# Windowed attention with a mixture of attention experts: tie mask, softmax path, one score block and the issue order

## The chip, the core and the metric

The kernel runs on one core of a Trainium2 chip. The metric is the time of one execution on the device in microseconds; of several runs the median counts. TensorE, VectorE, ScalarE and GpSimd work side by side on tiles in SBUF, TensorE writes to eight banks of PSUM, and SyncE issues nearly all transfers between HBM and SBUF. In the profile these are PE, DVE, ACT, POOL and SP; PEld is TensorE's weight load.

## What is computed

The first part is attention of 8 batches with 8 heads, 576 positions and 64 columns a head, in which each query sees its own and the 63 positions before it. Its output, 512 columns a position, goes into a mixture of four causal attention experts. A gate picks the two best experts for each position and weighs them. The core of the reference in outline:

```python
# first part: q, k, v are (8, 8, 576, 64)
scores = scale * np.matmul(q, k.transpose(0, 1, 3, 2))
mask = (rel >= 0) & (rel < window)            # window = 64
attn = softmax(np.where(mask, scores, -1e9))
x = np.matmul(attn, v)                        # to (8, 576, 512)

# second part
logits = x @ w_gate                           # 4 experts
topk = np.argpartition(-logits, 2, axis=-1)[..., :2]
w = softmax of the two chosen logits
for e in range(4):
    q, k, v = x @ wq[e], x @ wk[e], x @ wv[e]
    a = softmax(causal(scale * (q @ k.T)))
    out += w of e (0 where e is not chosen) * (a @ v @ wo[e])
```

## The kernel before

**First part.** The work is cut into 576 tiles, each of 64 queries of a pair of heads, and eight tiles make a unit u; there are 36 units. `s1_qk` (L379) multiplies queries by keys (TensorE, plain fp32), and builds the softmax in a tile `sm1_u`: ScalarE and a predicated copy on VectorE bring the scores from PSUM to SBUF, VectorE takes the maximum into `st1_u`. From there two paths lead on. A biased unit (odd u below 12, L408) lets ScalarE take the exponential of each of the eight tiles with its own bias, with the sum read from ScalarE's accumulator. Every other unit has GpSimd add the negative maximum, ScalarE take one exponential of the whole, and VectorE reduce the sum. VectorE's reciprocal and GpSimd's product follow. `s1_t` (L424) transposes the result on TensorE (t1), masks it into pt1; `s1_av` multiplies by the values (o1) and writes the output as two fp32r tiles, XH (rounded) and XL (the rest).

**Second part.** It runs in 16 halves (b, pr), a batch and a pair of experts. `s2_v` projects values and gate logits (v2ps), `s2_gate` (L598) builds the gate weights, `s2_k` and `s2_q` (L646, L657) project keys and queries (kps, qps). A product of this part is three fp32r products, hi·hi, hi·lo and lo·hi (`three`, L569). From the projected keys come KT, a high part that ScalarE copies and a low part that VectorE subtracts, and KF, the first 64 columns in plain fp32; queries likewise give QT and QF. `s2_mm` (L676) computes the scores in four steps k. Query block i holds queries 128i-64 to 128i+63, and step 0 holds block 1 with 192 keys and block 2 with 320 keys. The two experts of a pair lie in different halves of the partitions, so their matmuls use different rows of the array. The first 64 queries go through QF and KF in plain fp32 (`s2_mm0`). `s2_soft` takes the minimum, the exponential and the weights, `s2_t` transposes on VectorE and moves blocks by 16 transfers, `s2_av_mm` multiplies by the values (o2), `s2_o` by wo (ops), and the result leaves.

**The gate's ties.** For each position and each pair of experts (e, f) `g4[:, 0]` says whether f's logit is greater than e's. The row sums are the ranks. Where two logits are equal, the lower number wins: `g4[:, 1]` says whether they are equal, GpSimd multiplies it by a constant `below` (1 where f < e) and adds it to `g4[:, 0]`. There are 12 calls: eight for four blocks of 128 positions at once (64 columns), four for a single block (16 columns).

**What sets the order.** Every engine call is recorded as a numbered operation, a matmul block as one, and issued in the order of a table of numbers, LIST (L29). So one table sets the order on every engine, SyncE's loads included. BANKS (L170) names the PSUM bank of each tile in the order of recording, and SLOTS (L178) the SBUF slot of each `sm1`, `ft` and `out` tile. All instructions come out of the same helper and carry its line, L218:

```python
for n in LIST:
    for call, args, kw in self.ops[n]:
        call(*args, **kw)
```

## Time and profile before

| | |
|---|---|
| time, median of 3 runs | 408.18 us (407.21 to 409.73) |
| profiled execution | 406.65 us |
| its span | 404.9 us |
| granted TensorE clock | 0.999 |
| TensorE busy | 395.0 us, 98% |
| VectorE busy | 304.9 us, 75% |
| ScalarE busy | 270.2 us, 67% |
| GpSimd busy | 266.4 us, 66% |

The span is the time from the first to the last recorded instruction or transfer of the profiled execution; 1.75 us lie around it. The shares are of the span. Matmuls are pipelined and overlap in the records, so the mean duration of a matmul is longer than the distance from one start to the next; where a step's price is meant, a row that holds a block of known count is read. A plain fp32 matmul stands in the records as two passes, an fp32r matmul as one. In the chain of waits and the list of waits, a name behind an arrow is what the waiting engine waited for.

### The profile page before, as it was taken

To read this page: it belongs to the slowest core of one execution; us is meant where nothing else is said; L and a number is where in the kernel's file an instruction comes from. 1 tells how busy PE (TensorE), PEld (TensorE's weight loads), DVE (VectorE), ACT (ScalarE), POOL (GpSimd) and SP (SyncE) were. 2 spreads that over 40 slices of the span, in tenths; PEclk is the share of its full clock that TensorE was granted. 3 is DMA by queue.
4 is the path that set the end of the run, shared out by engine and by line. 5 is a ranking of instruction groups with operands and counts; after the bars stand their busy time and mean duration, and the time that the engine had idled before them with its cause. 6 is when DMAs were issued, how large, how long until landed. Compare 5 with 4: busy or idle time off the path is not lost.

```text
span 404.9 us, 14099 instructions
## 1 busy us (share of the span) xinstructions
PE 395.0 (98%) x5316; PEld 357.1 (88%) x5316; DVE 304.9 (75%) x989; ACT 270.2 (67%) x960; POOL 266.4 (66%) x465
## 2 busy tenths in 40 slices
PE   7799999999999999999999999999999999999995
PEld 6589989999888999889988999989998999988884
DVE  4899999978987688767886868968786748386632
ACT  4889888758576585946676575757657473748842
POOL 3756658897879666977677767887668663506300
PEclk9999999999999999999999999999999999999999
DMA  7998335565867573687957574378646630645024
GB/s 223 344 398 298 122 91 204 142 202 156 266 210 230 117 233 137 152 267 210 295 141 196 154 211 197 89 188 314 169 122 163 168 78 22 145 129 145 2 90 159
DMA packets 34132, 72.70 MB, mean 180 GB/s; under 512 B 6544, under 2 KB 11152, under 8 KB 34064
## 3 DMA queue, kind: packets, MB, share of 16 engines
q1 hardware_dynamic: 33408, 71.14, 58.2%
q8 instruction: 42, 0.69, 0.7%
q10 hardware_dynamic: 656, 0.66, 0.6%
q14 instruction: 26, 0.21, 0.2%
HBM read 39.85 MB, written 9.44 MB: 122 GB/s over the span
## 4 chain that ended last, share of the span: by engine, by line
PE 90%; DMA 3%; ACT 3%; DVE 2%; SPq 1%; issue 0%
PE o L218 20%; PE s L218 16%; PE ops L218 13%; PE v2ps L218 12%; PE qps L218 12%; PE kps L218 12%; PE t L218 4%; DMA v<-in_vW_dram 2%; ACT sm L218 2%; DMA q<-in_qT_dram 1%; DVE p L218 1%; SPq L218 1%; PE warm L218 1%; DVE pt L218 1%; ACT ft L218 0%
## 5 line engine op out<-in xcount | busy, mean ns | idle before, releaser
L218 POOL TENSOR_SCALAR_AFFINE_SELECT pt<-ft 64x512 f32<-64x512 f32 x126 | 83.2, 664 | 35.4 <-ACT ft L218 24.5
L218 POOL TENSOR_SCALAR p<-p,r,g 128x448 f32<-128x448 f32 (+3 forms) x135 | 83.6, 632 | 18.0 <-DVE r L218 15.8
L218 ACT ACTIVATE p<-p,r 128x320 f32<-128x320 f32 (+4 forms) x135 | 78.2, 585 | 13.1 <-DVE r L218 12.9
L218 PE MATMUL o<-pt,v 128*64 128x64 f32 (+2 forms) x1776 | 80.2, 248 | 0.8 <-DVE gt L218 0.3
L218 PEld LDWEIGHTS o<-pt,v 128*64 128x64 f32 x1776 | 68.0, 138 | 13.4 <-issue 1.7
L218 POOL TENSOR_TENSOR sm<-sm,st 128x512 f32<-128x512 f32 x66 | 68.3, 1044 | 13.5 <-DVE st L218 6.6
L218 DVE STREAM_TRANSPOSE st<-p 128x128 f32<-128x128 f32 (+5 forms) x126 | 60.7, 515 | 7.7 <-DMA pt<-st 5.1
L218 DVE CUSTOM_DVE_ANT_0 p<-s,causal 128x320 f32<-128x320 f32 (+2 forms) x120 | 53.4, 484 | 7.4 <-PE s L218 6.9
L218 DVE TENSOR_REDUCE st<-sm 128x8 f32<-128x512 f32 x66 | 44.3, 678 | 5.8 <-ACT sm L218 5.0
L218 PE MATMUL s<-kt,qt 64*128 64x320 f32 (+3 forms) x480 | 41.7, 315 | 0.0
L218 PE MATMUL qps<-xh,wqhi 128*128 128x320 f32 (+1 forms) x128 | 39.1, 306 | 0.0
L218 PE MATMUL s<-k,q 64*64 64x128 f32 (+1 forms) x1116 | 36.2, 267 | 2.3 <-DMA q<-in_qT_dram 2.1
L218 PE MATMUL kps<-xh,wkhi 128*128 128x320 f32 (+1 forms) x128 | 38.2, 299 | 0.0
L218 PE MATMUL qps<-xl,wqhi 128*128 128x320 f32 (+1 forms) x128 | 37.7, 294 | 0.0
L218 PE MATMUL qps<-xh,wqlo 128*128 128x320 f32 (+1 forms) x128 | 37.6, 294 | 0.0
L218 PE MATMUL kps<-xh,wklo 128*128 128x320 f32 (+1 forms) x128 | 37.6, 294 | 0.0
L218 PE MATMUL kps<-xl,wkhi 128*128 128x320 f32 (+1 forms) x128 | 37.6, 294 | 0.0
L218 PE MATMUL v2ps<-wvhi,xh 128*128 128x260 f32 x128 | 37.3, 291 | 0.0
L218 DVE COPY_PREDICATED sm<-own,s 128x256 f32<-128x256 uint8 x72 | 29.5, 438 | 9.0 <-ACT sm L218 7.9
L218 PE MATMUL v2ps<-wvhi,xl 128*128 128x260 f32 x128 | 36.1, 282 | 0.0
L218 PE MATMUL v2ps<-wvlo,xh 128*128 128x260 f32 x128 | 36.1, 282 | 0.0
L218 PEld LDWEIGHTS s<-kt,qt 64*128 64x128 f32 x480 | 34.6, 186 | 1.7 <-issue 0.4
(126 smaller groups left out, 939.8 us busy)
## 6 DMA issues: line engine op xcount, KB each, us to landing
v<-in_vW_dram SPq DMA_DIRECT2D x28, 576.0 KB, 6.2
pt<-st SPq DMA_DIRECT2D x112, 116.0 KB, 2.3
pt<-st SPq DMA_DIRECT2D x112, 80.0 KB, 2.1
out_dram<-out SPq DMA_DIRECT2D x32, 256.0 KB, 2.5
q<-in_qT_dram SPq DMA_DIRECT2D x28, 288.0 KB, 5.4
k<-in_kT_dram SPq DMA_DIRECT2D x28, 288.0 KB, 5.2
v<-in_vW_dram SPq DMA_DIRECT2D x3, 320.0 KB, 7.1
out_dram<-out SPq DMA_DIRECT2D x7, 128.0 KB, 2.5
```

Source lines behind the costliest of these rows:

```text
L218: call(*args, **kw)
```

## The change

1. **Gate.** `is_equal` becomes `is_ge`, and the two GpSimd operations give way to one predicated copy on VectorE: where `lower`, a byte copy of `below` that is made once, is set, `g4[:, 0]` is overwritten with the result of `is_ge`.
2. **Softmax path.** The biased units are 1, 3 and 5 instead of 1, 3, 5, 7, 9 and 11. Units 7, 9 and 11 take the path with the add on GpSimd, one exponential and the reduction on VectorE.
3. **Scores of queries 64 to 191** (block 1, 192 keys): one plain fp32 product from QF and KF instead of three fp32r products from QT and KT, for each expert. QF and KF grow from 64 to 192 columns, QT shrinks from 512 to 384, so in the first half of the query projection the high copy and the low subtraction have 128 columns less.
4. **Order.** LIST, BANKS and SLOTS are new, planned with SyncE held at instruction fetches.

```diff
--- before.py
+++ after.py
@@ -27,157 +27,156 @@
 CPOS = 0.202
 OLATE = 1.7
 LIST = (
-    6, 7, 5, 3, 4, 0, 2, 15, 1, 81, 241, 34, 35, 14, 40, 43, 42, 50, 48, 52, 51, 17, 16, 19, 20, 21, 18, 78, 12, 77,
...
+    34, 35, 46, 51, 53, 4, 5, 1, 3, 7, 45, 50, 54, 44, 52, 15, 6, 14, 48, 77, 47, 78, 0, 84, 80, 82, 109, 55, 2, 17,
...
 )
 BANKS = (
-    "7032162174036526122706545743666144303575372011542742670750361363436234076521457174625011572302605261"
...
+    "6041263030541725674120645630334724751702705154362052776756651563442650220632342525246031572750247301"
...
 )
 SLOTS = (
-    "3300536326421402533610362513401135536262401140433102626545450431245606020232065454133415540621650436"
...
+    "1601335122430463562135612053465543341211603120013225440613416615050426555200264154360432461531324062"
...
 )
 TAIL = 2
 WARM = 16
@@ -405,7 +404,7 @@
             nc.vector.copy_predicated(sm[:, x], own[:, None, :].to_broadcast([128, w, 64]), banks[x][:, 0:w, 64:128])
         flat = sm.rearrange("r x j c -> r (x j) c")
         nc.vector.tensor_reduce(st[:, 0], flat, axis=AX.X, op=OP.max, negate=True)
-        if u < 12 and u % 2:
+        if u in (1, 3, 5):
             nc.scalar.activation(st[:, 0], st[:, 0], AF.Copy, scale=0.125)
             for t in range(n):
                 nc.scalar.activation(flat[:, t], flat[:, t], AF.Exp, bias=st[:, 0, t:t + 1], scale=0.125,
@@ -513,10 +512,10 @@
 
 
     L = [const.tile([128, 5, E], F32, name=f"logits{i}") for i in range(2)]
-    QT = [const.tile([128, 2, 512], F32R, name=f"qt{i}") for i in range(2)]
+    QT = [const.tile([128, 2, 384], F32R, name=f"qt{i}") for i in range(2)]
     YH = [const.tile([128, S + 64], F32R, name=f"yh{i}") for i in range(2)]
     YL = [const.tile([128, S + 64], F32R, name=f"yl{i}") for i in range(2)]
-    QF = [const.tile([128, 64], F32, name=f"qf{i}") for i in range(2)]
+    QF = [const.tile([128, 192], F32, name=f"qf{i}") for i in range(2)]
     G2 = [const.tile([128, 2, 9], F32, name=f"g2_{i}") for i in range(2)]
     KT, KF, R2, M2 = {}, {}, {}, {}
 
@@ -545,6 +544,7 @@
 
     causal = const.tile([128, 576], F32, name="causal")
     below = const.tile([128, E, E], F32, name="below")
+    lower = const.tile([128, E * E], mybir.dt.uint8, name="lower")
 
     def stage2_constants():
         for h in range(2):
@@ -562,6 +562,7 @@
         nc.gpsimd.memset(below, 0.0)
         for e in range(1, E):
             nc.gpsimd.memset(below[:, e, 0:e], 1.0)
+        nc.vector.tensor_copy(lower, below.rearrange("r e f -> r (e f)"))
 
     def clear_pt2():
         nc.gpsimd.memset(PT2.rearrange("r (a f) -> r a f", a=4)[64:128, :, FF:FS], 0.0)
@@ -603,9 +604,9 @@
         lf = lg[:, :, None, :].to_broadcast([128, n, E, E])
         le = lg[:, :, :, None].to_broadcast([128, n, E, E])
         nc.vector.tensor_tensor(g4[:, 0], lf, le, op=OP.is_gt)
-        nc.vector.tensor_tensor(g4[:, 1], lf, le, op=OP.is_equal)
-        nc.gpsimd.tensor_tensor(g4[:, 1], g4[:, 1], below[:, None].to_broadcast([128, n, E, E]), op=OP.mult)
-        nc.gpsimd.tensor_tensor(g4[:, 0], g4[:, 0], g4[:, 1], op=OP.add)
+        nc.vector.tensor_tensor(g4[:, 1], lf, le, op=OP.is_ge)
+        first, ties = (g4[:, x].rearrange("r j e f -> r j (e f)") for x in range(2))
+        nc.vector.copy_predicated(first, lower[:, None, :].to_broadcast([128, n, E * E]), ties)
         gt = work.tile([128, 3, 4, E], F32, tag="gt", name=f"gt_{b}_{j0}")[:, :, :n]
         gs = work.tile([128, 3, 4], F32, tag="gs", name=f"gs_{b}_{j0}")[:, :, :n]
         nc.vector.tensor_reduce(gt[:, 0], g4[:, 0], axis=AX.X, op=OP.add)
@@ -647,8 +648,8 @@
 
         ps, c0, n = proj(b, "k", pr, half)
         if half == 0:
-            KF[b, pr] = work.tile([128, 64], F32, tag="kf", name=f"kf_{b}_{pr}")
-            nc.scalar.activation(KF[b, pr], ps[:, :64], AF.Copy)
+            KF[b, pr] = work.tile([128, 192], F32, tag="kf", name=f"kf_{b}_{pr}")
+            nc.scalar.activation(KF[b, pr], ps[:, :192], AF.Copy)
             KT[b, pr] = work.tile([128, 2, S], F32R, tag="kt", name=f"kt_{b}_{pr}")
         hi, lo = (KT[b, pr][:, x, c0:c0 + n] for x in range(2))
         nc.scalar.activation(hi, ps, AF.Copy)
@@ -656,13 +657,13 @@
 
     def s2_q(b, pr, half):
         ps, c0, n = proj(b, "q", pr, half)
-        x0 = 64 if half == 0 else 0
-        d = slice(c0 + x0 - 64, c0 + n - 64)
+        x0 = 192 if half == 0 else 0
+        d = slice(c0 + x0 - 192, c0 + n - 192)
         hi, lo = (QT[pr][:, x, d] for x in range(2))
         nc.scalar.activation(hi, ps[:, x0:], AF.Copy)
         nc.vector.tensor_sub(lo, ps[:, x0:], hi)
         if half == 0:
-            nc.scalar.activation(QF[pr], ps[:, :64], AF.Copy)
+            nc.scalar.activation(QF[pr], ps[:, :192], AF.Copy)
 
 
     SCORES = (((1, 0, 192), (2, 0, 320)), ((3, 0, 448),), ((4, 0, 320),), ((4, 320, 256),))
@@ -678,7 +679,13 @@
                                 for e in range(2)]
         with nc.block("1234"[k]):
             for i, key, n in SCORES[k]:
-                q = slice(128 * i - 128, 128 * i)
+                if i == 1:
+                    for e in range(2):
+                        r = slice(64 * e, 64 * e + 64)
+                        nc.tensor.matmul(banks[e][:, at(i, e):at(i, e) + n], lhsT=QF[pr][r, 64:192],
+                                         rhs=KF[b, pr][r], start=True, stop=True)
+                    continue
+                q = slice(128 * i - 256, 128 * i - 128)
                 for x, (w, m) in enumerate(((0, 0), (0, 1), (1, 0))):
                     for e in range(2):
                         r = slice(64 * e, 64 * e + 64)
@@ -689,7 +696,7 @@
         with nc.block("0"):
             for e in range(2):
                 r = slice(64 * e, 64 * e + 64)
-                nc.tensor.matmul(SB[b, pr, 1][0][r, 448:512], lhsT=QF[pr][r], rhs=KF[b, pr][r], start=True, stop=True)
+                nc.tensor.matmul(SB[b, pr, 1][0][r, 448:512], lhsT=QF[pr][r, :64], rhs=KF[b, pr][r, :64], start=True, stop=True)
 
     def s2_soft(b, pr, k):
         if k == 0:
```

**TensorE, the scores of batch 4's first half** (s2_4_0_k_e is step k for expert e, kt and qt the fp32r keys and queries, t1_25 a transpose of the first part). Before:

```order
L218 MATMUL s2_4_0_2_0_687<-kt_4_0_651,qt0_88 128x320
L218 MATMUL s2_4_0_2_1_688<-kt_4_0_651,qt0_88 128x320
L218 MATMUL s2_4_0_0_0_683<-kt_4_0_651,qt0_88 128x192
L218 MATMUL s2_4_0_0_1_684<-kt_4_0_651,qt0_88 128x192
L218 MATMUL s2_4_0_0_0_683<-kt_4_0_651,qt0_88 128x192
L218 MATMUL s2_4_0_0_1_684<-kt_4_0_651,qt0_88 128x192
L218 MATMUL s2_4_0_0_0_683<-kt_4_0_651,qt0_88 128x192
L218 MATMUL s2_4_0_0_1_684<-kt_4_0_651,qt0_88 128x192
L218 MATMUL s2_4_0_0_0_683<-kt_4_0_651,qt0_88 128x320
L218 MATMUL s2_4_0_0_1_684<-kt_4_0_651,qt0_88 128x320
```

After (kf and qf are the plain fp32 keys and queries):

```order
L217 MATMUL t1_25_0_642<-ident_85,sm1_25_612 128x64
L217 MATMUL t1_25_1_643<-ident_85,sm1_25_612 128x64
L217 MATMUL s2_4_0_0_0_684<-kf_4_0_651,qf0_94 128x192
L217 MATMUL s2_4_0_0_1_685<-kf_4_0_651,qf0_94 128x192
L217 MATMUL s2_4_0_0_0_684<-kt_4_0_652,qt0_88 128x320
L217 MATMUL s2_4_0_0_1_685<-kt_4_0_652,qt0_88 128x320
L217 MATMUL s2_4_0_0_0_684<-kt_4_0_652,qt0_88 128x320
L217 MATMUL s2_4_0_0_1_685<-kt_4_0_652,qt0_88 128x320
L217 MATMUL s2_4_0_0_0_684<-kt_4_0_652,qt0_88 128x320
L217 MATMUL s2_4_0_0_1_685<-kt_4_0_652,qt0_88 128x320
L217 MATMUL t1_26_0_646<-ident_85,sm1_26_618 128x64
```

The six fp32r rows of 192 columns are two plain rows. What stands beside them also moved: before, step 2 stood ahead of them, now the transposes of unit 25 do, and unit 26's transposes follow.

**VectorE, the last low part of kt_0_1**, the keys of batch 0's second half (st2<-p2 are transposes of batch 0's first half, g4, gt and gs the gate, st1_11 the statistics of unit 11). Before:

```order
L218 TENSOR_TENSOR g4_0_4_279<-logits0_86 128x16
L218 TENSOR_TENSOR qt1_89<-qps_0_1_1_283,qt1_89 128x320
L218 STREAM_TRANSPOSE st2_69<-p2_0_67 128x2x2x32
L218 TENSOR_REDUCE gt_0_4_280<-g4_0_4_279 128x4
L218 TENSOR_TENSOR kt_0_1_236<-kps_0_1_1_282,kt_0_1_236 128x320
L218 STREAM_TRANSPOSE st2_69<-p2_0_67 128x4x4x32
```

After:

```order
L217 TENSOR_REDUCE gs_0_4_282<-gt_0_4_281 128x1
L217 TENSOR_SCALAR gs_0_4_282<-gs_0_4_282 128x1
L217 STREAM_TRANSPOSE st2_69<-p2_0_67 128x2x2x32
L217 RECIPROCAL gs_0_4_282<-gs_0_4_282 128x1
L217 STREAM_TRANSPOSE st2_69<-p2_1_68 128x6x4x32
L217 TENSOR_REDUCE st1_11_251<-sm1_11_250 128x8
L217 STREAM_TRANSPOSE st2_69<-p2_1_68 128x2x2x32
L217 TENSOR_TENSOR kt_0_1_237<-kps_0_1_1_283,kt_0_1_237 128x320
```

The subtraction stood ahead of the transpose of 128x4x4x32 columns. Now that transpose (further ahead than the rows shown), the one of 128x6x4x32 and the reduction for unit 11's sum stand ahead of it.

**TensorE, ahead of the first projection v2ps_0_0** (s1_7 and s1_8 are scores of units 7 and 8, which read the load k7; t1_3 the transposes of unit 3). Before:

```order
L218 MATMUL s1_8_1_210<-k7_171,q7_170 64x128 x2
L218 MATMUL s1_8_0_209<-k7_171,q7_170 64x128 x2
L218 MATMUL s1_8_1_210<-k7_171,q7_170 64x128 x2
L218 MATMUL t1_3_155<-ident_85,sm1_3_145 128x128 x4
L218 MATMUL v2ps_0_0_208<-wvhi_180,xh0_128 128x260
```

After, where t1_3 stands now, and where the projection follows the scores:

```order
L217 MATMUL t1_3_156<-ident_85,sm1_3_146 128x128 x4
L217 MATMUL s1_7_0_196<-k6_151,q6_150 64x128 x2
L217 MATMUL s1_7_1_197<-k6_151,q6_150 64x128 x2
L217 MATMUL s1_7_0_196<-k6_151,q6_150 64x128 x2
L217 MATMUL s1_7_1_197<-k6_151,q6_150 64x128 x2
```

```order
L217 MATMUL s1_8_0_210<-k7_172,q7_171 64x128 x2
L217 MATMUL s1_8_1_211<-k7_172,q7_171 64x128 x2
L217 MATMUL s1_8_0_210<-k7_172,q7_171 64x128 x2
L217 MATMUL s1_8_1_211<-k7_172,q7_171 64x128 x2
L217 MATMUL v2ps_0_0_209<-wvhi_181,xh0_129 128x260
```

The transposes of unit 3 moved from behind the scores of units 7 and 8 to ahead of them.

## Rows read from the trace of the kernel before

**Rows 1.** The page's busy line: engine, us busy (share of the span), instructions.

```profile
PE 395.0 (98%) x5316; PEld 357.1 (88%) x5316; DVE 304.9 (75%) x989; ACT 270.2 (67%) x960; POOL 266.4 (66%) x465
```

**Rows 2.** TensorE's waits, whole run: who waited for whom, us in total, times, longest.

```profile
PE s L218 <- DMA q<-in_qT_dram: 2.1, 3, 1.1
PE warm L218 <- POOL ident L218: 1.6, 1, 1.6
```

**Rows 3.** TensorE's waits from 27 to 400 us, longest of three.

```profile
PE o L218 <- DVE gt L218: 0.3, 1, 0.3
```

**Rows 4.** Stretches: us, busy us of each engine, clock, DMA share, GB/s.

```profile
50.00:60.00 10.00, 9.46 (x214) 8.38 (x212) 9.80 (x39) 7.54 (x28) 6.20 (x13) 1.00 0.27 76
...
100.00:200.00 100.00, 99.76 (x1411) 91.01 (x1409) 78.64 (x260) 67.01 (x232) 76.97 (x133) 1.00 0.70 205
```

**Rows 5.** TensorE's groups by form: operation, tile, count, busy us, mean ns.

```profile
L218 PE MATMUL o<-pt,v 128*64 128x256 f32 x240 | 31.5, 383 | 0.2 <-DVE kt L218 0.2
...
L218 PE MATMUL o<-pt,v 128*64 128x128 f32 x120 | 11.8, 274 | 0.0
...
L218 PE MATMUL s<-kt,qt 64*128 64x192 f32 x96 | 8.3, 277 | 0.0
```

**Rows 6.** The chain that ended last: start us, us, engine, tile, count.

```profile
131.04 0.98 PE s L218 x12
...
254.61 1.61 PE qps L218 x12
...
259.06 0.99 PE s L218 x12
...
287.42 1.41 PE qps L218 x12
```

**Rows 7.** TensorE's timeline near 250 us: start us, us, operation, tile, shape, count.

```profile
250.23 0.40 PE L218 MATMUL ops<-wolo,yh 128*128 128x512 f32 x1
250.46 0.40 PE L218 MATMUL ops<-wohi,yl 128*128 128x512 f32 x1
250.79 0.46 PE L218 MATMUL t<-ident,sm 64*128 64x64 f32 x8
251.06 1.63 PE L218 MATMUL s<-kt,qt 64*128 64x192 f32 x18
```

**Rows 8.** VectorE's timeline near 67 us.

```profile
66.67 0.47 DVE L218 TENSOR_TENSOR kt<-kps,kt 128x320 fp32r<-128x320 f32 x1
```

**Rows 9.** TensorE's timeline near 69 us.

```profile
68.60 1.64 PE L218 MATMUL s<-kt,qt 64*128 64x448 f32 x18
```

**Rows 10.** SyncE's timeline: the load of k7.

```profile
18.91 0.33 SPq L218 DMA_DIRECT2D k<-in_kT_dram  x1
```

**Rows 11.** Transfers issued at that moment: count, KB each, us to landing.

```profile
k<-in_kT_dram SPq DMA_DIRECT2D x1, 288.0 KB, 6.1
```

**Rows 12.** The timeline of all engines ahead of the first projection.

```profile
23.77 1.05 POOL L218 TENSOR_TENSOR sm<-sm,st 128x512 f32<-128x512 f32 x1
...
24.97 1.64 PE L218 MATMUL s<-k,q 64*64 64x128 f32 x51 [0.22 <-issue]
...
26.55 0.66 PE L218 MATMUL t<-ident,sm 128*128 128x128 f32 x4
...
26.96 0.36 PE L218 MATMUL v2ps<-wvhi,xh 128*128 128x260 f32 x1
```

**Rows 13.** VectorE's groups by form: busy us, mean ns, idle before.

```profile
L218 DVE TENSOR_REDUCE st<-sm 128x8 f32<-128x512 f32 x66 | 44.3, 678 | 5.8 <-ACT sm L218 5.0
L218 DVE COPY_PREDICATED sm<-own,s 128x256 f32<-128x256 uint8 x72 | 29.5, 438 | 9.0 <-ACT sm L218 7.9 <-POOL g L218 0.3
...
L218 DVE TENSOR_TENSOR qt<-qps,qt 128x256 fp32r<-128x256 f32 x28 | 11.3, 410 | 4.3 <-ACT qt L218 4.2
...
L218 DVE TENSOR_TENSOR g<-logits 128x64 f32<-128x64 f32 x16 | 4.5, 302 | 4.1 <-ACT logits L218 4.1
```

**Rows 14.** GpSimd's groups by form: the larger gate product.

```profile
L218 POOL TENSOR_TENSOR g<-g,below 128x64 f32<-128x64 f32 x8 | 2.6, 325 | 12.7 <-DVE g L218 11.3 <-DVE gs L218 1.1
```

More of the change, by code (lines that the diff above doesn't have):

```diff
@@ L29 @@
 LIST = (
[139 rows of a table removed]
[138 rows of a table added]
 )
 BANKS = (
-    "7032162174036526122706545743666144303575372011542742670750361363436234076521457174625011572302605261"
-    "0454140613306447132046562545302774061225054361320153706724144234660343046216142637554672333105732015"
-    "1352077264276103547141412536207375434070247164250346126034303502160473527746156412155723730461501045"
-    "5036374146027105166063027367404042537612207527131556716214157150736437242500061047535764213751045676"
-    "5042363406427450332720160536711010463752462414561232135464651056247124433523731467125056541726725763"
-    "41"
+    "6041263030541725674120645630334724751702705154362052776756651563442650220632342525246031572750247301"
+    "0546427017651773702037410654276336770162312514021525140436266462440563102754560457373516000212350607"
+    "0453235413734510262476152041372226757405724213676023710336163574605346524207145767514706203601741247"
+    "1216745277233771175232436256110404163376573176430254601447645460325255543317217076306501752051645152"
+    "7562012404372473014276116657534014705236412730475066127354321250113471601164352737423520305472540476"
+    "21"
 )
 SLOTS = (
-    "3300536326421402533610362513401135536262401140433102626545450431245606020232065454133415540621650436"
-    "12540325"
+    "1601335122430463562135612053465543341211603120013225440613416615050426555200264154360432461531324062"
+    "51606543"
 )
```

275 rows, old and new, of the table LIST are left out of this document.

## Prediction

> **What bounds the kernel now.** I read the page's busy line first, then TensorE's waits, then the stretches, and only then single rows. TensorE is busy 395.0 of 404.9 us [rows 1], VectorE 304.9, so the time is TensorE's work plus what little it idles. The reader should see in the waits that nearly all of TensorE's waiting lies at the start: 2.1 us for the first queries and 1.6 us for the constant the warm-up multiplies by [rows 2]. From 27 to 400 us there are three waits in all, 0.2 to 0.3 us each, 0.7 us in sum, and none on a transfer [rows 3]. The stretches say the same: TensorE is busy 9.46 of 10 us from 50 to 60, and 99.76 of 100 us from 100 to 200 [rows 4]. So after 27 us a better order alone can win about 1 us, and an edit that spares VectorE, ScalarE or GpSimd wins only where TensorE waits for that engine. That place is 50 to 60 us, where VectorE is busy 9.80 of 10 us [rows 4]; later it has slack (78.64 of 100). The sum below is made against the profiled execution, 406.65 us, which is 1.53 below the median of the runs (408.18); I add that at the end.
>
> **The plain product for queries 64 to 191.** Per half and expert three fp32r steps of 192 columns go, and a plain fp32 product that shows as two passes comes; the two experts use different rows of the array and run side by side. The old price: the block of twelve with 192 and 320 columns takes 0.98 us, the block with 320 and 256 columns 0.99 [rows 6]. So 64 columns less save nothing; the 192-column step costs what the 256-column step costs. That is 0.117 us: twelve 256-column steps take 1.41 us [rows 6]. Three steps: 0.35 us. The new price: plain fp32 passes of 256 and 128 columns last 383 and 274 ns [rows 5], 109 ns for 128 columns, 0.85 ns a column. Two passes of 192: 0.33 us. So a half gains 0.02 and all 16 gain 0.4 us. The bounds: if the old steps went by columns (0.42 ns, half the plain pass's 0.85) they took 3 × 0.08 = 0.24 us and the change loses 0.09 × 16 = 1.4 us; if the new pass costs what the old step does (2 × 0.117) it gains 0.12 × 16 = 1.8 us. I take -0.4, since both prices come from blocks of this kind. The mean duration of the 192-column form, 277 ns [rows 5], isn't its price: matmuls overlap.
>
> The Trainium skill, "FP8 and Floating Point Precision", section "TensorE Precision Notes", has true FP32 take 4 passes over the array. By columns that is four of 0.08 us against three, or 1.3 us more in sum, where the rows give 0.4 less. The trace agrees with four for the new product (two records at twice the column price) but not with the three by columns for the old one. This is a rival below.
>
> **Changes of tile shape.** A change of TensorE's tile shape costs: twelve projection steps take 1.61 us behind a score block and 1.41 behind another projection [rows 6], 0.20 us. A change of number format with the same 64-row shape shows nothing: eight plain fp32 transposes start at 250.79 and the fp32r scores behind them at 251.06 [rows 7], which is 0.034 us a transpose with nothing left for a pause; ahead of these transposes, where the shape changes too, 0.33 us pass against the 0.23 of a step before [rows 7]. The new product keeps the 64×128 shape of its neighbours (the first place of the order), so it costs no pause. Counted over the whole order there are 125 changes of shape instead of 123: +0.4 us.
>
> **Gate.** The 12 calls lose two GpSimd operations each, of 0.3 us in the large calls [rows 14], and VectorE gains a predicated copy in each; is_ge takes the place of is_equal at one price. The copy is not in the trace at this size. The nearest rows are the comparison of the same shape, 302 ns, and a predicated copy of 256 columns, 438 ns [rows 13]. Between nothing and 12 × 0.44 = 5.3 us I take 0.30 each: 3.6 us. No wait of TensorE after 27 us names a gate operation on GpSimd [rows 3], so what GpSimd saves gains nothing directly.
>
> **Biased units.** Units 7, 9 and 11 move their sum from ScalarE to VectorE: one reduction of 678 ns each [rows 13], +2.0 us on VectorE; ScalarE loses 24 short exponentials with their accumulator reads, GpSimd gains three adds. All three are scored ahead of 60 us, where VectorE is full.
>
> **Copies.** The low-part subtraction for queries has 128 columns less in 16 halves. The 256-column one lasts 410 ns [rows 13]; halving its columns saves between nothing and half: 0 to 3.3 us, I take 2.1. ScalarE's copies grow by 128 columns, which ScalarE, relieved above, absorbs. In sum VectorE gets 3.6 + 2.0 - 2.1 = 3.5 us more of work (bounds -1.3 to 7.3), 1% of its 304.9. After 100 us its slack covers that.
>
> **Where it is not covered.** VectorE's part of this ahead of 70 us is the three reductions, two gate copies and the cast of the new mask, about 2.5 us, in a stretch that has 0.2 us of slack in 10 [rows 4]. The second place of the order shows who is late: the last low part of kt_0_1 now stands behind two large transposes and the reduction of unit 11. Before it started at 66.67 and lasted 0.47 [rows 8], and TensorE began the scores that read it at 68.60 [rows 9]: a lead of 1.46 us. Adding the durations of before along each order, VectorE's work ahead of it grows by 5.5 us and TensorE's work ahead of those scores by 3.6. The lead falls by 1.9 and turns into a wait of 0.5 us; the scores themselves stand later, so behind them only work that doesn't hang on it is queued. I take +0.6, bounds 0 (VectorE had idle time there to take up) and +2.5 (all that is added lands on TensorE).
>
> **The start.** The first projection, v2ps_0_0, began at 26.96 [rows 12]. Ahead of it stand the scores of unit 8, which began at 24.97 [rows 12], when k7 had landed: issued at 18.91 [rows 10], 6.1 us to landing [rows 11]. In the new order of loads as many bytes stand ahead of k7, so I let it land at the same time. The transposes t1_3 stood between the scores and the projection and now stand ahead of the scores (third place of the order), in time that waits for the load. Their input was multiplied on GpSimd from 23.77 for 1.05 us [rows 12], too late for that, but the reciprocal of unit 3, VectorE's step ahead of it, now comes before the long subtraction for wv's low part instead of behind it. The transposes took the time from 26.55 to 26.96 [rows 12], 0.4 us: I take -0.4, bounds -0.6 and 0.
>
> **The other stalls.** The order is new everywhere, so the idle 0.54 us of 50 to 60 and 0.24 of 100 to 200 [rows 4] may go or come again elsewhere. I take -0.5, bounds 0 and -1.0. SyncE: TensorE waits for no transfer after 27 us [rows 3], so what the order does for SyncE has little left to win.
>
> **The sum.** -0.4 (start) - 0.4 (product) + 0.4 (shapes) + 0.6 (VectorE) - 0.5 (stalls) = -0.3: 406.35 us beside 406.65, which is 407.9 by the median. A measurement of this kernel can tell about 1% from no change (4.1 us: below 404.1 or above 412.3), so this is no change.
>
> **The rivals.**
> - *Plain fp32 between fp32r makes TensorE stop (the other side).* If the format change costs like a shape change, each of the 16 blocks, between fp32r or differently shaped rows, pays 2 × 0.20 us [rows 6]: +6.4, 414.3 us, slower. It decides from 0.26 us a block on. For it speaks that no plain product of this shape stands there before; against it the transposes of [rows 7]. The Trainium skill, "TensorEngine Tiling (Array Packing)", section "Key Properties", has a change of tiling mode drain TensorE and says nothing of formats; the rows agree. Chance 0.06.
> - *VectorE becomes the bound from 30 to 100 us.* The 2.5 us land on TensorE, and a second late consumer adds as much: +2 to +4 beyond the forecast, 410 to 412 us. For it speaks 9.80 of 10; against it that TensorE idled only 0.54 us there. Chance 0.12.
> - *The four-pass rule by columns.* The old steps were worth 0.24 us a half and the new ones 0.33: +1.4 in place of -0.4, 409.7 us. Against it stand 0.98 and 0.99 [rows 6]. Chance 0.05.
> - *The new order takes up the stalls.* Half of the start's 3.7 us [rows 2] (-1.9), all of the 1.0 us after it, and no VectorE term: 406.65 - 0.4 + 0.4 - 1.9 - 1.0 = 403.75, or 405.3 by the median, and 403.9 if the product also gains its bound of 1.8. Chance 0.12.
> - *No change, as summed*, with its bounds 406 to 409.7: chance 0.65.
>
> **How the numbers follow.** Predicted 407.9. The range reaches from 404.3, inside the case of the stalls, to 411.0, inside VectorE's; outside stay the stop for formats (0.06), a third of VectorE's case (0.04) and a third of the stalls' (0.04), some 0.15 with the noise of the runs. Faster than 404.1: a third of the stalls' case, and a share for an order that does more than I see in the rows: 0.10. Slower than 412.3: the stop for formats and VectorE's end: 0.08. Within 1%: 0.82.
>
> **What would show it.** The plain passes between the scores of a half should start about 0.16 us apart with no gap ahead or behind; a gap of 0.2 us or more at all 16 places proves the first rival. The wait of scores for kt's low part near 70 us should be new and under 1 us; several waits for VectorE from 40 to 100 us prove the second. v2ps_0_0 should start near 26.5. The GpSimd gate operations go and TensorE's waits don't show it. The prediction is wrong if TensorE's busy time itself changes by over 2 us, or if TensorE waits on loads after 27 us.

## The result, and the profile after

Over eight runs each, the changed kernel's median is 409.98 us (408.48 to 410.71) and that of the kernel before 408.02 (406.86 to 409.73). The ratio is 1.0055 with an interval of 1.0036 to 1.0074: slower by half a per cent, some 2.2 us, where I forecast 0.3 us less. Here and below a difference in us is worked out from the ratio and the median of the kernel before beside it; it can lie some tenths off the difference of the two medians. The change is inside the 1% that I called no change, but the interval excludes my sign. Three later measurements of the unaltered changed kernel, each beside the kernel before on one chip, gave 1.0029, 1.0038 and 1.0024, none of whose intervals holds 1. So the change costs 1.0 to 2.2 us.

Busy time in the profile after (it answers to [rows 1]):

```profile
PE 398.7 (98%) x5284; PEld 360.7 (88%) x5284; DVE 305.7 (75%) x1005; ACT 265.9 (65%) x912; POOL 265.4 (65%) x444
```

The span is 408.8 us, 3.9 longer than before, and TensorE is busy 3.7 us longer although it has fewer matmuls; that is one of the signs that the prediction named for being wrong (over 2 us). TensorE's waits, first of the whole span (to [rows 2]), then from 27 to 400 us alone (to [rows 3]); total us, times, longest:

```profile
PE s L217 <- DMA q<-in_qT_dram: 4.2, 3, 3.4
```

```profile
PE o L217 <- DVE pt L217: 0.5, 1, 0.5
PE o L217 <- DVE r L217: 0.2, 1, 0.2
PE t L217 <- DVE sm L217: 0.2, 1, 0.2
```

After 27 us there are again three waits, 0.9 us against 0.7. At the start the longest wait for queries is 3.4 us. The stretches (busy us with instructions of PE, PEld, DVE, ACT, POOL; PEclk, the granted clock; DMA share; GB/s), first two of the kernel before, then those after:

```profile
10.00:20.00 10.00, 7.56 (x128) 5.40 (x122) 8.60 (x19) 8.00 (x36) 7.24 (x9) 1.00 1.01 340
20.00:30.00 10.00, 9.78 (x182) 8.68 (x180) 9.40 (x17) 8.89 (x32) 5.60 (x10) 1.00 1.04 400
```

```profile
10.00:20.00 10.00, 6.00 (x85) 4.38 (x88) 6.73 (x16) 6.70 (x32) 5.60 (x8) 0.82 0.98 317
20.00:30.00 10.00, 10.00 (x199) 8.37 (x193) 8.42 (x16) 9.14 (x33) 5.95 (x11) 0.84 1.04 356
30.00:40.00 10.00, 10.00 (x130) 9.61 (x128) 9.93 (x19) 7.57 (x33) 8.15 (x10) 1.00 0.61 209
40.00:50.00 10.00, 9.32 (x169) 8.62 (x169) 9.84 (x24) 6.87 (x22) 6.82 (x8) 1.00 0.84 290
50.00:60.00 10.00, 10.00 (x136) 9.08 (x134) 9.88 (x34) 6.14 (x20) 8.83 (x16) 1.00 0.01 3
```

VectorE is full from 30 to 60 us (9.84 to 9.93 of 10), and yet TensorE is busy 10.00 of 10 us in two of these three stretches; the third, from 40 to 50, has the wait of 0.5 us. What got worse lies ahead of 30 us: TensorE idles 4.0 us from 10 to 20 instead of 2.4, and the granted clock is 0.82 and 0.84 instead of 1.00. The rows of that place, TensorE's and SyncE's (SPq) from the timeline after:

```profile
10.91 0.43 SPq L217 DMA_DIRECT2D q<-in_qT_dram  x1
...
16.97 1.13 PE L217 MATMUL s<-k,q 64*64 64x64 f32 x16 [3.38 <-DMA q<-in_qT_dram]
...
19.07 1.97 PE L217 MATMUL s<-k,q 64*64 64x128 f32 x32
...
21.03 0.43 SPq L217 DMA_DIRECT2D k<-in_kT_dram  x1
...
23.29 1.10 PE L217 MATMUL s<-k,q 64*64 64x128 f32 x32
...
27.47 0.65 PE L217 MATMUL t<-ident,sm 128*128 128x128 f32 x4
28.05 1.96 PE L217 MATMUL s<-k,q 64*64 64x128 f32 x64
29.97 0.38 PE L217 MATMUL v2ps<-wvhi,xh 128*128 128x260 f32 x1
```

The load of q4 is issued at 10.91, and unit 4's scores wait for it 3.38 us. In the old order four transposes (t1_0) stood ahead of those scores; now they stand behind. From 16.97 on TensorE has no idle time up to v2ps_0_0, but works at half speed for 6 us: the block of 32 score steps at 19.07 takes 1.97 us and its like at 23.29 takes 1.10. v2ps_0_0 starts at 29.97 instead of 26.96 [rows 12].

The granted clock (third figure from the end) in steps of 2 us, after:

```profile
14.00:16.00 2.00, 0.00 (x0) 0.00 (x0) 1.93 (x6) 1.17 (x4) 1.82 (x4) 1.00 0.99 298
16.00:18.00 2.00, 1.03 (x16) 0.76 (x16) 0.43 (x2) 0.00 (x0) 1.60 (x2) 0.60 1.00 327
18.00:20.00 2.00, 2.00 (x25) 1.65 (x27) 1.33 (x3) 1.58 (x7) 0.09 (x1) 0.50 1.05 390
20.00:22.00 2.00, 2.00 (x25) 1.67 (x20) 1.41 (x3) 1.43 (x10) 1.84 (x3) 0.50 1.09 362
```

Behind the idle piece the clock is at its lower level, 1.2 GHz (0.50), for some 6 us. k7's load, too, is issued at 21.03 instead of 18.91 [rows 10]: q7 and k7 take the buffers of q4 and k4, so their loads wait for unit 5's scores, which read q4 last. SyncE's waits for TensorE's scores, 5 to 24 us, after (0.7 us in sum before):

```profile
SPq L217 <- PE s L217: 2.7, 2, 2.3
```

The theory was then: the three edits cost about what the sum said, and the loss lies in the start. The rival: the edits cost much more than summed, and the new order pays for them. Both turned out to hold in part.

### The profile page after: what moved, and what is told of

Read it like the earlier page. It is cut to its first block, busy times and chain, and to the rows that moved or that the text cites. A ratio compares the mean times of both kernels' runs of the same rounds, so it can differ in the third digit from the quotient of the medians.

```text
span 408.8 us, 13988 instructions
## 1 busy us (share of the span) xinstructions
PE 398.7 (98%) x5284; PEld 360.7 (88%) x5284; DVE 305.7 (75%) x1005; ACT 265.9 (65%) x912; POOL 265.4 (65%) x444
## 4 chain that ended last, share of the span: by engine, by line
PE 93%; DMA 3%; DVE 2%; SPq 0%; issue 0%; ACT 0%
PE o L217 20%; PE s L217 17%; PE v2ps L217 13%; PE kps L217 13%; PE ops L217 12%; PE qps L217 12%; PE t L217 5%; DMA q<-in_qT_dram 2%; DMA k<-in_kT_dram 1%; DVE pt L217 1%; SPq L217 0%; PE warm L217 0%; DVE xl L217 0%; DVE st L217 0%; DVE wolo L217 0%; DVE wqlo L217 0%
## 5 line engine op out<-in xcount | busy, mean ns | idle before, releaser
L217 POOL TENSOR_SCALAR p<-p,r,g 128x320 f32<-128x320 f32 (+4 forms) x135 | 83.7, 631 | 25.7 <-DVE r L217 20.2
L217 POOL TENSOR_TENSOR sm<-sm,st 128x512 f32<-128x512 f32 x69 | 72.2, 1056 | 22.9 <-DVE st L217 21.0
L217 PEld LDWEIGHTS o<-pt,v 128*64 128x64 f32 x1776 | 69.3, 138 | 12.7 <-issue 2.1
L217 DVE TENSOR_REDUCE st<-sm 128x8 f32<-128x512 f32 x69 | 45.7, 675 | 4.2 <-ACT sm L217 3.6
L217 PE MATMUL s<-kt,qt 64*128 64x320 f32 (+2 forms) x384 | 41.1, 336 | 0.0
L217 PE MATMUL qps<-xh,wqhi 128*128 128x256 f32 (+1 forms) x128 | 38.6, 302 | 0.0
L217 PEld LDWEIGHTS s<-k,q 64*64 64x64 f32 x1116 | 31.4, 138 | 7.0 <-issue 5.0
L217 PE MATMUL qps<-xl,wqhi 128*128 128x256 f32 (+1 forms) x128 | 37.6, 294 | 0.0
L217 PE MATMUL qps<-xh,wqlo 128*128 128x256 f32 (+1 forms) x128 | 37.6, 294 | 0.0
L217 ACT ACTIVATE sm<-s 128x256 f32<-128x256 f32 (+3 forms) x88 | 25.3, 328 | 16.9 <-PE s L217 14.7
```

## The experiments

### The edits one by one in the old order

**All three edits with before's LIST, BANKS and SLOTS.** The cast of `lower` stands right behind the last write of `below`.

```diff
 LIST, BANKS, SLOTS: those of the kernel before
+is_ge, copy_predicated, lower; units 1, 3, 5 biased; plain product for queries 64 to 191
```

> All three edits (gate, units 7, 9 and 11, plain product) in the order, the banks and the slots of the kernel before; what the edits add stands where the instructions stood that they replace. Theory A (the loss is the new order's start, where TensorE idles 3.4 us for q4, its clock falls and the first projection starts 3.0 us late): the edits alone cost nothing, 407.0 to 408.3, first projection near 27.0, clock 1.00 throughout. Theory B (the loss is the edits: VectorE's added work, or the plain product): near 410, with new waits of TensorE for VectorE between 40 and 100 us.

Measured: 414.77 us, ratio 1.0180 (1.0159 to 1.0201): 7.3 us slower. Both expectations (up to 408.3, and near 410) were too low. TensorE's longest three waits from 27 to 400 us, and the place of the cast:

```profile
PE o L217 <- POOL pt L217: 0.9, 2, 0.6
PE qps L217 <- DVE sm L217: 0.9, 1, 0.9
PE kps L217 <- DVE st L217: 0.9, 1, 0.9
```

```profile
42.89 1.04 POOL L217 TENSOR_TENSOR sm<-sm,st 128x512 f32<-128x512 f32 x1
42.97 1.00 DVE L217 CAST lower<-below 128x16 uint8<-128x16 f32 x1 [1.07 <-POOL below L217]
...
44.36 0.42 PE L217 MATMUL qps<-xh,wqhi 128*128 128x320 f32 x1 [0.86 <-DVE sm L217]
```

So the edits are dear where they meet an order that was not made for them. The cast of 16 columns waits 1.07 us for `below`, then lasts 1.00 us beside a GpSimd product of 1.04, and the projection behind it waits 0.86.

**The plain product alone.**

```diff
 s2_mm, kernel before
+                if i == 1:
+                    one plain product from QF and KF, columns 64 to 191
 QF, KF 192 columns, QT 384
```

> The kernel before with the plain product for queries 64 to 191 alone, order unchanged. By the prediction's price (0.35 us down to 0.33 a half): 407.6, that is -0.4. If plain fp32 between fp32r stops TensorE: +6.4, 414.4. By the four-pass rule with steps that go by columns: +1.4, 409.4. Theory A has it at 407 to 408.3; theory B, if the product is the cause, near 410.

Measured: 407.27 us, 1.0003 (0.9989 to 1.0016). Neither the stop for formats (+6.4 us would be 1.016) nor the four-pass rule by columns (+1.4, 1.0034) fits.

**The biased units alone** (7, 9 and 11 over GpSimd and VectorE, old order):

```diff
-        if u < 12 and u % 2:
+        if u in (1, 3, 5):
```

> The kernel before, its order kept, with only the softmax path of units 7, 9 and 11 changed (add on GpSimd, one exponential, sum on VectorE, each where the biased path's first and last instructions stood). All edits together in the old order took 414.8, the plain product alone 407.3. If the units are the cause of the 7.5 us: 412 to 414, with new waits of TensorE for VectorE and GpSimd between 30 and 80 us. If it is the gate: 407 to 408.

Measured: 410.35 us, 1.0082 (1.0064 to 1.0101): 3.3 us, between the two expectations. TensorE's waits from 27 to 400 us, the longest three:

```profile
PE kps L217 <- DVE st L217: 1.0, 1, 1.0
PE o L217 <- POOL pt L217: 0.7, 2, 0.5
PE kps L217 <- DVE sm L217: 0.5, 1, 0.5
```

Two of them are for VectorE's reduction or copy, one for GpSimd. I had priced 2.0 us on VectorE and nothing on the way over GpSimd.

**The gate alone**, the cast just ahead of the first copy that reads it:

```diff
-        nc.vector.tensor_tensor(g4[:, 1], lf, le, op=OP.is_equal)
-        nc.gpsimd.tensor_tensor(... mult)
-        nc.gpsimd.tensor_tensor(... add)
+        nc.vector.tensor_tensor(g4[:, 1], lf, le, op=OP.is_ge)
+        nc.vector.copy_predicated(first, lower..., ties)
```

> The kernel before, its order kept, with only the gate changed: predicated copy where GpSimd's add stood, and the byte mask made just ahead of the first gate's copy (not behind GpSimd's constant, where the run of all edits had VectorE wait 1.07 us for it). If the gate costs only its instructions (12 copies of 0.2 to 0.4 us, a cast of 1.0): 407 to 408.5. If the gate is the cause of the 7.5 us: 411 to 414.

Measured: 409.51 us, 1.0061 (1.0044 to 1.0077): 2.5 us, more than its expectation (407 to 408.5) and under that of the gate as the whole cause. VectorE's forms here, and those of the changed kernel (total us, mean ns):

```profile
L218 DVE COPY_PREDICATED g<-lower,g 128x64 f32<-128x64 uint8 x8 | 1.8, 231 | 0.2
...
L218 DVE CAST lower<-below 128x16 uint8<-128x16 f32 x1 | 0.2, 157 | 0.0
```

```profile
L217 DVE TENSOR_TENSOR qt<-qps,qt 128x128 fp32r<-128x128 f32 x14 | 4.0, 288 | 4.3 <-ACT qt L217 4.2
L217 DVE COPY_PREDICATED g<-lower,g 128x64 f32<-128x64 uint8 x8 | 3.0, 375 | 0.2
...
L217 DVE CAST lower<-below 128x16 uint8<-128x16 f32 x1 | 1.0, 1018 | 0.0
```

The copy is cheap (231 ns) and the cast cheaper (157); in the new order they last 375 and 1018. The two edits and the product, 2.5, 3.3 and 0.1 us, make 5.9 of the 7.3. What the other 1.4 us are isn't shown; one difference is the cast, which stands elsewhere in gate_only.

TensorE's order is that of the kernel before in these kernels, so the place of the loss can be read from the traces. From v2ps_0_0 to the first product by wo (ops) pass 82.70 us before, 82.97 with the plain product, 84.06 with the gate, 86.61 with the units and 89.55 with all edits; from v2ps_0_0 to the end of the span 377.97, 378.06, 380.26, 381.86 and 385.45. So of the 7.5 us that all edits add behind v2ps_0_0, 6.9 arise ahead of that product, and little behind it.

**VectorE's time by itself.** The kernel before, the maximum of units 7, 9 and 11 taken twice: 3 × 0.68 us more on VectorE, nothing moved, no longer way.

```diff
+        if u in (7, 9, 11):
+            nc.vector.tensor_reduce(st[:, 0], flat, axis=AX.X, op=OP.max, negate=True)
```

> The kernel before with one thing added: the maximum of units 7, 9 and 11 is taken twice, 3 x 0.68 us more on VectorE at the place where the changed softmax path adds its sums, nothing else moved. The units' path alone in this order cost 3.4 us. If VectorE's work is what costs there: +1.5 to +2.5, 408.5 to 409.5. If it is the longer chain through GpSimd and VectorE of those units: under +0.7. What is left of the 3.4 us is the chain's share.

Measured: 408.69 us, 1.0032 (1.0019 to 1.0045): 1.3 us (0.8 to 1.8 by the interval) for 2.0 us of work. So ahead of 60 us about two thirds of VectorE's added time land on the end. Of the units' 3.3 us that leaves, by difference, some 2.0 for the longer way over GpSimd; it was not measured by itself.

**The old units in the new order.**

```diff
 the changed kernel
-        if u in (1, 3, 5):
+        if u < 12 and u % 2:
```

> The changed kernel with units 7, 9 and 11 biased again, in the new order. If the units' VectorE work is what the new order still pays for between 27 and 100 us (0.9 us more lost there than before): 409.0, about 0.5 to 1 under the changed kernel. If the loss is the start alone: no change against the changed kernel, 409.7 to 410.2 or its value in this call. If ScalarE, with its longer queue, is late in the new order: slower than the changed kernel.

Measured: 411.66 us, 1.0110 (1.0093 to 1.0127), where the control beside it has 1.0029. Undoing an edit that costs 3.3 us in the old order costs 3.3 us in the new one. Each order fits its own edits.

### The start

**The control.** The changed kernel unaltered, three times.

> The changed kernel once more, as a control beside these runs, with its profile: 409.5 to 410.5, or 1.0055 times the kernel before. Theory A (the clock falls in TensorE's idle piece near 14 us): the profiled execution again shows a granted clock under 0.9 from 16 to 24 us if its time is above the median, and 1.00 if it is below.

> The changed kernel as the control for the first and the fourth run of this call: 1.003 to 1.0055 times the kernel before.

> The changed kernel unaltered, as a control beside these two: 408.3 to 410.0 us by the medians so far, ratio to the kernel before 1.003 to 1.0055, v2ps_0_0 between 27.7 and 30.0 us, span that start plus 378.5 to 378.9.

Measured: 408.33, 408.95 and 408.08 us (1.0029, 1.0038, 1.0024), the first below its expectation. Their first projections, one profile each:

```profile
27.67 0.39 PE L217 MATMUL v2ps<-wvhi,xh 128*128 128x260 f32 x1 [0.24 <-DVE xl L217]
```

```profile
28.73 0.38 PE L217 MATMUL v2ps<-wvhi,xh 128*128 128x260 f32 x1 [0.30 <-DVE xl L217]
```

```profile
27.61 0.39 PE L217 MATMUL v2ps<-wvhi,xh 128*128 128x260 f32 x1 [0.31 <-DVE xl L217]
```

The spans are 406.2, 407.6 and 406.4; less these starts 378.5, 378.9 and 378.8, and 378.8 in the first profile. Before it was 404.9 - 26.96 = 377.9. Against that one profile of before the start is 0.7 to 3.0 us late and is paid in full, and from v2ps_0_0 to the end the changed kernel loses 0.6 to 1.0 us. The idle pieces ahead of unit 4's scores were 3.38, 2.67, 2.6 and 1.40 us long, and the clock of 10 to 20 us was 0.82 to 0.85 in all four: executions of one kernel differ here by more than my start term. The execution profiled in the first control was faster than that control's median and had the half clock too, where I had expected 1.00.

The start of before scatters as well. The five kernels above with the old order issue the same instructions ahead of v2ps_0_0 as before, and there it starts at 27.88 (all edits), 27.21 (plain product), 26.38 (units), 27.64 (gate) and 28.01 (maximum twice). The earliest and the latest row:

```profile
26.38 0.37 PE L217 MATMUL v2ps<-wvhi,xh 128*128 128x260 f32 x1
```

```profile
28.01 0.37 PE L219 MATMUL v2ps<-wvhi,xh 128*128 128x260 f32 x1
```

With before's 26.96 that is 26.4 to 28.0 us in six executions of the old start, 27.3 in the mean, and 27.6 to 30.0 in four of the new, 28.5 in the mean. The new start is some 1.1 us later by these means, but the two overlap, and the 3.0 us of the first profile are its far end.

What is lost behind v2ps_0_0 is TensorE's busy time. The whole stretch from there to the end, before and in the first control:

```profile
26.96:404.93 377.97, 373.01 (x4921) 339.29 (x4919) 285.48 (x949) 251.96 (x892) 251.16 (x427) 1.00 0.57 170
```

```profile
27.67:406.25 378.58, 374.12 (x4884) 339.98 (x4884) 287.69 (x965) 247.62 (x842) 250.59 (x404) 1.00 0.57 170
```

The other three have 374.30 to 374.35. TensorE's idle time up to its last matmul is 0.8 us before and 0.8 to 0.9 in the four, and behind that matmul 4.2 us pass before and 3.6 in the four.

**q4's load earlier.**

```diff
 (order of SyncE)
+k4<-in_kT_dram, q4<-in_qT_dram
 v0<-in_vW_dram, st2<-in_vW_dram
-k4<-in_kT_dram, q4<-in_qT_dram
```

> The changed kernel with one move on SyncE: the loads of k4 and q4 stand ahead of the first parts of v0 and of the fourth pair's values instead of behind them. Theory A: q4 lands 1.5 to 2 us earlier, TensorE's idle piece near 14 us falls from 3.4 to under 2 us, the clock stays at 1.00, the first projection starts near 27, and 2 to 3 us of the time come back: 407.3 to 408.3. Theory B: unchanged, near 410.

> The changed kernel with the loads of k4 and q4 ahead of the values, again, now beside its control. Theory A: the clock stays at 1.00 and the time is 0.5 to 1.5 us under the control. Rival (the late first projection is bound by k7's load and by unit 0's product on GpSimd as well, 27.9 in the first run of this kernel against 27.7 in a run of the changed kernel): within 0.4 us of the control.

Measured: 408.98 and 408.87 us, 1.0043 and 1.0035; beside the second the control had 1.0038. That is above the 407.3 to 408.3 expected of the theory. In the first profile the clock was 1.00 throughout, and yet:

```profile
26.47 1.23 PE L217 MATMUL s<-k,q 64*64 64x64 f32 x36 [0.96 <-DMA k<-in_kT_dram]
27.88 0.39 PE L217 MATMUL v2ps<-wvhi,xh 128*128 128x260 f32 x1 [0.18 <-DVE xl L217]
```

With q4's wait down to 0.60 us, k7's landing was next. The second profile had its idle piece elsewhere (2.33 us for the queries one load earlier) and v2ps_0_0 at 28.75. No gain.

**Work in the idle piece.** Unit 4's scores are split, and 15 products of the warm-up constant, which change no result, stand ahead of the part that reads q4.

```diff
 (order of TensorE)
+warm_0<-ident x15
 s1_4<-k4,q4
```

> The changed kernel with TensorE kept busy in the idle piece: unit 4's scores are split in two blocks, and the warm-up product that stood ahead of them stands between them, 15 times instead of once (about 3.2 us of work that nobody reads). Loads and order stay. If the clock is the larger part of the late start: granted clock 1.00 from 16 to 24 us, s1_5 done near 18.7 instead of 20.6, k7's load issued 1.7 us earlier, first projection near 28.3, time 408.3 to 408.8. If the late load alone makes it: unchanged, 409.7 to 410.2. Theory B: unchanged.

Measured: 408.97 us, 1.0049 (1.0029 to 1.0068). TensorE's clock stayed at 1.00, and v2ps_0_0 began at 28.27 as worked out, but a new idle piece came, by the stretch and the timeline:

```profile
20.00:22.00 2.00, 0.79 (x24) 0.55 (x24) 1.86 (x4) 2.00 (x12) 1.80 (x4) 1.00 1.10 371
```

```profile
22.26 0.45 PE L217 MATMUL s<-k,q 64*64 64x64 f32 x8 [1.47 <-DMA q<-in_qT_dram]
```

TensorE now waited 1.47 us for the next queries. The time lies a little above the 408.3 to 408.8 expected if the clock were the larger part, and no lower than the controls: keeping the clock up gave nothing back.

**Before's start, the new rest.** The first 190 operations in the order of before.

```diff
 LIST
-the first operations of the changed kernel
+the first 190 operations as in the kernel before, then the rest of the changed one
```

> The changed kernel, all edits kept; its first 190 operations (loads, units 0 to 7, to the scores that read k6) stand in the order of the kernel before, everything behind them in the new order; banks and slots moved only where two tiles would meet. Theory A (the start costs 0.6 to 2.9 us, the rest 0.9): first projection at 26.4 to 27.2, granted clock 1.00 throughout, idle in front of q4 under 1 us, time 0.8 to 2 us under the changed kernel beside it, that is at most 0.9 us above the kernel before. Rival: what is gained at the start is lost again before 60 us, because VectorE is the bound there (9.8 of 10 us busy): within 0.3 us of the changed kernel.

Measured: 410.67 us, 1.0086 (1.0063 to 1.0110), slower than its control (1.0038) where I had expected less, and v2ps_0_0 at 31.20 in the profile. TensorE stood idle for 1.88 us up to 27.04 and ScalarE for 2.1 us for VectorE's statistics, between the last old row and the first new ones. Spliced like this the old start can't be had; whether another splice does better wasn't tried.

**wv's chain earlier.** The 8 KB load of the gate's weights right behind wv's load instead of behind wk's; wvhi and wvlo ahead of the first xh and xl, as before; in the second kernel also q4's load first.

```diff
 (order of SyncE; wvhi on ScalarE and wvlo on VectorE likewise)
 pt2<-in_wv_dram
+pt2<-in_wg_dram
 k6, q6, v1, v2, pt2<-in_wk_dram
-pt2<-in_wg_dram
```

> The changed kernel, with the 8 KB load of the gate's weights moved from behind wk's load to just behind wv's, and with wvhi (ScalarE) and wvlo (VectorE) moved ahead of the low parts of the first attention outputs, as in the kernel before; nothing is left out. Theory (the start's last link is wg's load, wvhi, wvlo, the second xl, v2ps_0_0): wvhi falls from 24.4 to 26.1 us in the three profiles of the changed kernel to about 20.5, the second xl follows its xh at once instead of behind wvlo's 1.5 to 1.8 us, and v2ps_0_0 comes 0.5 to 1 us earlier than in the control beside it (27.7 to 30.0); the span stays v2ps_0_0's start plus 378.7, the median falls by 0.5 to 1 us against the control. Rival (the start is held by the unit 8 scores, which wait for k7, and by the half clock): the second xl is early, TensorE doesn't wait for it, v2ps_0_0 and the median stay as in the control.

> The kernel wv_early, with the loads of k4 and q4 ahead of the first two loads of v as well (as in q4_first). Theory (three links hold the start, each behind the other: q4's load, wg's with wvhi and wvlo, k7's behind the scores of unit 5): with the first two moved v2ps_0_0 starts at about 27.5 instead of 27.9 to 28.8 in q4_first, held by k7, and the median is about 1 us below the control, within 0.5 us of the kernel before. Rival (the loads' sum of bytes sets the start, whatever their order): v2ps_0_0 stays near 28 to 28.7 and the median within 0.5 us of the control.

Measured: 409.58 us, 1.0063 (1.0041 to 1.0085), and 408.2, 1.0030 (1.0018 to 1.0043), where the control has 408.08 and 1.0024 (1.0008 to 1.0040). The first is slower than its control, the second equals it. Rows of wv_early:

```profile
22.64 1.24 DVE L217 SCALAR_TENSOR_TENSOR wvlo<-pt,wvhi 128x1040 fp32r<-128x1040 f32 x1
...
26.39 1.28 DVE L217 TENSOR_TENSOR xl<-o,xh 128x512 fp32r<-128x512 f32 x2
...
26.55 0.66 PE L217 MATMUL t<-ident,sm 128*128 128x128 f32 x4 [1.04 <-POOL sm L217]
...
27.14 1.96 PE L217 MATMUL s<-k,q 64*64 64x128 f32 x64
...
29.03 0.19 PEld L217 LDWEIGHTS v2ps<-wvhi,xh 128*128 128x128 f32 x1 [0.17 <-issue]
```

wvlo and xl are early, the wait for xl is gone, and v2ps_0_0 is no earlier: TensorE stands at t1_3, which waits 1.04 us for GpSimd's product, and behind t1_3 all 64 score steps of units 7 and 8 (1.9 us) still come ahead of the projection. In before these scores stood ahead of t1_3 and ran while its input was made. The rival that I had written beside this run held in its outcome, not in its reason: no row waits for k7 here.

## Why the prediction was right and wrong

**The plain product: right.** Pass after pass starts 0.16 us apart as forecast. The timeline after at one half:

```profile
56.21 0.71 PE L217 MATMUL s<-kt,qt 64*128 64x320 f32 x6
56.75 0.49 PE L217 MATMUL s<-kf,qf 64*128 64x192 f32 x4
56.94 0.74 PE L217 MATMUL s<-kt,qt 64*128 64x320 f32 x6
57.52 0.41 PE L217 MATMUL t<-ident,sm 64*128 64x64 f32 x8
```

From 56.75 to 57.52 pass 0.77 us; a pair of 320-column steps takes 0.146 us in the single records, three of them 0.44, which leaves 0.33 for the plain product, the price in the sum. plain_only's interval holds the -0.4 of the sum and excludes both TensorE rivals.

**Gate, units and copies: the work right, its price a matter of the order.** The reductions came at 678 ns, the query subtractions save 1.9 us in sum of my 2.1, the gate copies at 375 ns in 8 calls and 288 in 4, 4.2 us of my 3.6. The cast, which I had put into 2.5 us without a price of its own, is 1.0 us. "After 100 us its slack covers that" holds in the main: in the old order 6.9 of 7.5 us arise ahead of the first product by wo, some 110 us into the span. For the stretch ahead of that the sum had 0.6 us, with a bound of 2.5; an order that was not made for the edits pays far more there. Alone, gate and units cost 2.5 and 3.3 us, and after the units' edit a projection waits 1.0 us for VectorE's reduction. That no wait of before named the gate's GpSimd part meant, as I now read it, that the old order hid it, not that its chain has room.

**The 0.6 for VectorE near 70 us: not seen.** No wait for kt's low part came; TensorE's waits after 27 us grew from 0.7 to 0.9 us. My terms other than the start make +0.1 (-0.4 + 0.4 + 0.6 - 0.5), and the time from v2ps_0_0 to the end grew by 0.6 to 1.0. It is 1.1 to 1.3 us more busy time of TensorE less 0.5 us at the end, not a wait for VectorE, so that 0.6 stands beside 0.6 is luck. The -0.5 for stalls did not come. Which instructions make the 1.1 to 1.3 wasn't taken apart.

**What the new order gives back: not seen.** All edits in the old order cost 7.3 us and in the new one 1.0 to 2.2. So the new order is worth 5 to 6 us to these edits, as placed here, and nothing in these runs is left over as a gain. The sum knew neither size: for the edits it had 0.6 - 0.4 and for the order -0.5 - 0.4. It reckoned VectorE's term on the new order, so the two belong together, but that it came out within 1% of the measurement is luck as to both.

**The start: the step that failed.** The sum took -0.4 us: the scores of unit 8 wait for k7, k7 lands when it did because as many bytes stand ahead of it, and t1_3 fills that wait. The first is what did not hold. In none of the four profiles of the changed kernel does TensorE wait for k7, not even in the first, where its load was issued 2.1 us later than before because q7 and k7 wait for unit 5's scores. TensorE was late itself: it stood 1.40 to 3.38 us for q4, worked at the lower clock (1.2 GHz) behind that, and then stood idle for at most 0.5 us up to v2ps_0_0, so that t1_3 had no wait to fill and took its time ahead of the scores, behind a wait for GpSimd of 0 to 0.2 us (1.04 in wv_early). v2ps_0_0 came 0.7 to 3.0 us later than in the profile of before, some 1.1 in the mean of all executions with either start, instead of 0.4 earlier. In the first profile that is 3.0 of 3.9 us. Over the four measurements it is about half, an estimate by difference: their ratios make 1.5 us in the mean, and some 0.8 us of that lie behind v2ps_0_0. Why the new start is late stays open: moving q4's load, the clock, wv's chain or two of these together gave nothing that the controls don't also show. t1_3's place was not tried alone.

**The rivals.** VectorE as the bound from 30 to 100 us is what happens in the old order, not in the changed kernel. The new order did not take up the start's stalls: TensorE's waits for queries were 4.2 us in the first profile, against 2.1. No kernel here beats the kernel before; the plain product alone equals it.

## What to carry over

An edit's price in a kernel with a planned order is measured twice, in the old order and in the planned one; the difference is what the order pays, and a list of waits of before can't show it, since the waits that the order hides aren't in it. Where an order of loads changes, follow for each load which buffer it reuses and whose reads it must wait for, not only the bytes ahead of it. Ask of each moved instruction what now stands behind it on its engine, and of a wait that it is to fill whether it is still there. Read a start from several executions: the same first instructions took 26.4 to 28.0 us here.

## What the hardware showed beyond that

**VectorE beside GpSimd.** The cast of 128x16 lasted 157 ns with GpSimd idle (gate_only) and 996 to 1018 in two other kernels; in the first of these the row of GpSimd's product from 42.89 for 1.04 us stands beside it, and both end together. In the changed kernel a product from 36.06 for 1.91 us stands beside the cast from 36.98 for 1.02. The gate's 16-column comparisons lasted 190 to 631 ns by order. The Trainium skill, "SBUF — State Buffer", section "Who interferes with whom", has a rule for this: a VectorE cast in its two-port mode, or an operation with two SBUF inputs, and a GpSimd operation that reads SBUF exclude each other for a whole instruction, and the later one blocks. The rows of edits_old_order agree; that the cast ran in that mode no row shows.

**The clock.** After an idle piece of 3.38 us TensorE was granted 0.50 to 0.60 of its clock for 6 us, and the same block took 1.97 us instead of 1.10. An idle piece of 1.40 us, with 0.94 a little ahead of it, was followed by the same: 0.83 from 10 to 20 us. One of 1.42 us in wv_early_q4_first was not: 1.00. With products in the idle piece the clock stayed at 1.00. In the six executions of the old start it was 1.00 from 10 to 20 us in five and 0.84 in one, with all edits; in the four of the changed kernel 0.82 to 0.85.
